# Where the weight splits of a fused attention and expert layer stand in their engines' queues

## The chip, the cores and the metric

The kernel runs on one core of a Trainium2 chip. The metric is the device time of one execution in microseconds (us). A core has five engines, each with a queue of its own: TensorE (PE) multiplies matrices, VectorE (DVE), ScalarE (ACT) and GpSimd (POOL) do elementwise work, SyncE (SP) issues the DMAs here.

## The reference

Two stages run one after the other. The first is attention with a decay per key, over 4 batches, 8 heads, 576 positions and a head size of 64. The second is a weighted sum of 4 dense experts over the 2304 rows of the attention's result, with 512 columns in and out and 1024 hidden columns.

```
scores = where(causal, -1e9, q @ k.T / sqrt(64) + cum[:, None] - cum[None, :])   # cum: running sum of log f
attn   = softmax(scores);  x = attn @ v                                          # then reshaped to (2304, 512)
h      = maximum(x @ w1[e], 0);  out += p[:, e] * (h @ w2[e])                    # e = 0..3, p normalized
```

All data are float32. The kernel keeps the precision by splitting an operand into a high part that TensorE can take and a low part (what is left), and by multiplying high by high, high by low and low by high.

## The kernel before

The result of the attention is cut into 9 chunks of 256 rows. The expert layer goes through chunks in small pieces that are called steps. A step is (s, g, c, ps): sweep s, group g of four weight units (two groups to an expert), chunk c, and ps, which of the two pairs of units of the group it uses. A unit is 128 hidden columns of one expert: 128x512 of w1 and 128x512 of w2, together 512 KB. Sweep 0 has the units 0 to 31 in a wide format, sweep 1 has the same weights again as units 32 to 63 in float16. `SWEEPS` says which chunks each sweep runs for each expert, and so how many chunks stand in a group: 1, 1, 2, 3 for the four experts of sweep 0, and 4, 4, 3, 2 for those of sweep 1. There are 28 steps in sweep 0 and 52 in sweep 1.

In the program's order, step n emits its first product (`l1`, 24 matmuls, line 1010), its gate (line 1023 on ACT takes the positive part as the high part, line 1024 on DVE makes the low part), and then the second product of step n-1 (`l2`, 12 matmuls, line 1043). Between these pieces `pace` emits slices of the attention for the chunks that come later: scores on PE (line 615), a running minimum on DVE (line 629), the exponential on ACT (line 644), normalized parts on ACT and DVE (lines 713 and 714), a transposing DMA, and the product with v (line 815). The preparation of a head is a copy of its q and k on ACT (line 562) and three instructions on POOL: line 563, line 571 (low part of k) and line 577 (low part of q), in `prep_lo`. Line 563 writes a buffer that the score matmuls of an earlier head read.

Each unit is loaded into one of three raw buffers (line 935, on SP's queue) and then split by `w_split`. For a unit of sweep 1 that is five instructions: line 977 on ACT and line 978 on DVE for the half of w1, line 969 on POOL, line 972 on ACT and line 973 on POOL for the half of w2. Splitting unit n also asks for the loads of units n+1 to n+3, and two steps later for the store of the split unit to DRAM (line 986), where the last stage of the kernel reads it again. For units of sweep 0 it is line 950 on ACT and line 954 on DVE or POOL.

The loop over steps asks for the split of two units when the last step that uses an older pair has been emitted: after the step in `ends[w0]`, units w0+6 and w0+7. The order in which instructions stand in each engine's queue is then set by a scheduler at build time: it simulates the engines with a cost model and takes, at each engine, what is ready first and was asked for first. So an instruction can come to stand in front of others that were asked for earlier. The engines run their queues in that order. `tc.issue_after(i)` tells the scheduler that what is emitted inside must stand behind instruction i in the queue of i's engine, if it is on that engine; it adds no instruction. Already used in the kernel before is this:

```python
def behind(f_):
    with tc.issue_after(prev.last.ins):
        f_()
```

After the steps, a last stage (`Big`, `Second`) computes the chunks 5 to 8 together, with weights that are read back from DRAM or summed anew on POOL (lines 1175, 1207, 1341). Its first two weight pairs are asked for early by `first_units`, after the steps of units 54 and 58; they use the raw buffers too.

Of the kernel before, what the change touches and what calls it, by code (L numbers as in the profile page):

```python
# [25 lines left out]
SWEEPS = (  # L26
    ((0,), (0,), (0, 1), (0, 1, 2)),
    ((1, 2, 3, 4), (1, 2, 3, 4), (2, 3, 4), (3, 4)),
)
# [7 lines left out]
LAST = (5, 6, 7, 8)  # L37
EARLY = (54, 58)
AHEAD = 4
W_SLOT = (4, 6)  # L40
NEAR = 2
JOBS = ((0, 0), (1, 0), (2, 0), (3, 0), (0, 1), (1, 1), (2, 1), (3, 1))
# [36 lines left out]
def fused(ctx: ExitStack, tc: tile.TileContext, qk, v, f, probs, w, out):  # L79
# [110 lines left out]
    def at_step(n, f):  # L190
        later.setdefault(n, []).append(f)
# [47 lines left out]
    def behind(f):  # L239
        if prev is None:  # L240
            f()
            return
        with tc.issue_after(prev.last.ins):
            f()
# [248 lines left out]
    class Job:  # L493
# [71 lines left out]
        def prep_lo(self, hh):  # L565
            if hh not in self.kl:
                self.rows(hh)
            wq, wk, ko, qo = self.wq, self.wk, self.ko, self.qo
            r, hi, kl = self.raw[hh], self.hi[hh], self.kl[hh]
            eng = nc.vector if self is jobs[0] else nc.gpsimd  # L570
            eng.tensor_tensor(  # L571
                out=kl[:64, :wk],
                in0=r[:64, ko : ko + wk],
                in1=hi[:64, ko : ko + wk].bitcast(F32),
                op=ALU.subtract,
            )
            eng.tensor_tensor(  # L577
                out=hi[64:128, qo : qo + wq],
                in0=r[64:128, qo : qo + wq],
                in1=hi[64:128, qo : qo + wq].bitcast(F32),  # L580
                op=ALU.subtract,
            )

        def prep(self, hh):
            self.prep_hi(hh)
            self.prep_lo(hh)
# [287 lines left out]
                )  # L874


    zs, pts = [], []
    jobs = []
    for b, half in JOBS:
        for pr in range(NPR):  # L880
# [51 lines left out]
    def w_load(n):  # L932
        if n < NS and n not in wraw:
            wraw[n] = wr_p.tile([128, 1024], F32, tag="wr", name=f"wr{n}")
            nc.sync.dma_start(out=wraw[n], in_=w[n % 32])
# [3 lines left out]
    def w_pair(name):  # L939
        t = w_p.tile([128, 2, 1024], F16, tag=("wh", "wl")[len(pairs) % 2], name=name)  # L940
        pairs.append(t)
        return t

    def w_split(n):
        w_load(n)
        r = wraw.pop(n)
        if n < 32:
            wh[n] = w_p.tile([128, 1024], F32R, tag="wh", name=f"wh{n}")
            wl[n] = w_p.tile([128, 1024], F32R, tag="wl", name=f"wl{n}")
            nc.scalar.activation(out=wh[n], in_=r, func=AF.Copy)  # L950
            eng = nc.vector if n in W_DVE else nc.gpsimd
            for a in (0, 512):
                z = a + 512
                eng.tensor_tensor(  # L954
                    out=wl[n][:, a:z],
                    in0=r[:, a:z],
                    in1=wh[n][:, a:z].bitcast(F32),
                    op=ALU.subtract,
                )
        else:  # L960
            e = n % 32 // 8
            assert ("w", e) in known
            t = w_pair(f"w{n}")
            wh[n], wl[n] = t[:, 0], t[:, 1]
            for k in range(2):
                c = slice(512 * k, 512 * k + 512)
                sc = wsc[:, e, k : k + 1]
                if k == 1:
                    nc.gpsimd.tensor_scalar(  # L969
                        out=r[:, c], in0=r[:, c], scalar1=sc, scalar2=None, op0=ALU.mult  # L970
                    )
                    nc.scalar.activation(out=wh[n][:, c], in_=r[:, c], func=AF.Copy)
                    nc.gpsimd.tensor_tensor(
                        out=wl[n][:, c], in0=r[:, c], in1=wh[n][:, c], op=ALU.subtract
                    )
                    continue
                nc.scalar.activation(out=wh[n][:, c], in_=r[:, c], func=AF.Copy, scale=sc)
                nc.vector.scalar_tensor_tensor(
                    out=wl[n][:, c],
                    in0=r[:, c],  # L980
                    scalar=sc,
                    in1=wh[n][:, c],
                    op0=ALU.mult,
                    op1=ALU.subtract,
                )
            at_step(step + 2, lambda: nc.sync.dma_start(out=wd[n - 32], in_=t))
        w_load(n + 1)
        w_load(n + 2)
        w_load(n + 3)
# [196 lines left out]
    def split_1(p):  # L1186
        if p >= 16:
            return ()
        r = raw_half(p, 0)
        t, u = (  # L1190
            w_p.tile([128, 2, 1024], F16, tag="wh", name=f"b{k}{p}") for k in ("w", "s")
        )
        one = t.rearrange("p n (s f) -> p n s f", s=2)
        for n in range(2):
            nc.sync.dma_start(out=one[:, n], in_=wd[2 * p + n][:, :, :512])
        bw[p] = one, u.rearrange("p s (k f) -> p s k f", k=4)
        f = sums(f"wt{p}", r, SUMS)
        hi, lo = u[:, 0], u[:, 1]

        def scale(a):  # L1200
            x = f[:, a : a + 512]
            nc.scalar.activation(out=x, in_=x, func=AF.Copy, scale=wsc[:, p // 4, 0:1])  # L1202

        def part(a):
            x, h = f[:, a : a + 512], hi[:, a : a + 512]
            nc.scalar.activation(out=h, in_=x, func=AF.Copy)  # L1206
            nc.gpsimd.tensor_tensor(out=lo[:, a : a + 512], in0=x, in1=h, op=ALU.subtract)  # L1207

        return (
            lambda: scale(0),  # L1210
            lambda: (part(0), scale(512)),
            lambda: part(512),
        )

    def first_units(w0):
        if w0 in EARLY:
            for f_ in split_1(EARLY.index(w0)):
                f_()
# [311 lines left out]
    def upto(n):  # L1530
        nonlocal at
        while at < n:
            asteps[at][1]()
            at += 1
# [6 lines left out]
    goals = sorted((max(n - LEAD, 1), cost[need[c]]) for c, n in first.items() if n > 0)  # L1541
    goals.append((len(steps) - AHEAD, cost[-1]))
    while goals:
# [17 lines left out]
    def startup():  # L1561
# [13 lines left out]
        for s in range(FIRST + 2):  # L1575
# [24 lines left out]
            if s >= 5 and s % 2 == 1:  # L1600
                heads[s - 4][0].fin()
            if s in W_SLOT:
                w_split(W_SLOT.index(s))

    prev, step = None, 0
# [8 lines left out]
    j.begin(0)  # L1614
    for n in range(len(W_SLOT), 6):
        w_split(n)

    used = set()
    for n in range(len(steps) + 1):
        step = n  # L1620
        cur = steps[n] if n < len(steps) else None
        for f_ in later.pop(n, ()):
            behind(f_)
        for e, first_ in enumerate(PEEK):
            if 0 <= n - first_ < 16:
                w_peek(e, n - first_)
            if n == first_ + 17:
                a_, b_ = w_scale(e)
                behind(a_)
                at_step(n + 3, b_)  # L1630
        if 0 <= n - V_PEEK < NV:
            v_peek(n - V_PEEK)
        if n == V_PEEK + NV + 1:
            a_, b_ = v_scale()
            behind(a_)
            at_step(n + 2, b_)
        if cur is not None:
            if cur.c not in used:
                used.add(cur.c)
                upto(need[cur.c])  # L1640
            for c, m in TURN:
                if n >= m and c not in yh and ("x", c) in known:
                    narrow(c)
            if cur.s == 1:
                assert cur.c in yh
                weigh(cur.g // 2, cur.c)
            for q in range(4):
                cur.l1(q)
                pace(n + q / 8)
            cur.gate()  # L1650
        else:
            upto(len(asteps))
            chunks.close()
            late.h = late.enter_context(tc.tile_pool(name="h", bufs=4, side="right"))
            for e in range(E):
                weigh(e, LAST[0])
            big = [Big(p) for p in range(16)]
            turns = in_turns(0)
            for _ in range(3):
                next(turns)()  # L1660
        if prev is not None:
            for q in range(4):
                prev.l2(q)
                pace(n + (q + 4) / 8)
                if cur is None:
                    for _ in range(2 if q == 3 else 1):
                        next(turns)()
            for w0, t in ends.items():
                if t is prev:
                    if w0 + 7 < NS:  # L1670
                        w_split(w0 + 6)
                        w_split(w0 + 7)
                    first_units(w0)
        prev = cur

    for p in range(2):
# [88 lines left out]
```

## Time and profile before

| what | value |
|---|---|
| time, median of 3 runs | 936.33 us (935.25 to 938.32) |
| profiled execution | 940.96 us, span 939.2 us |
| mean granted TensorE clock | 0.976 |
| busy in the span: PE, DVE, ACT, POOL | 884.8, 718.5, 567.5, 523.7 us (94, 77, 60, 56%) |
| sweep 0, sweep 1, last stage | to about 240 us, to about 625 us, to the end |

The table is from the page of one profiled execution. Busy is the time in which an engine executes; a wait for a semaphore is idle time of the engine. In the rows further down, what stands in square brackets behind an instruction is the time that its engine sat idle in front of it and the instruction that released it. A granted clock of 1.00 is 2.4 GHz, 0.50 is 1.2 GHz, and what is between is a mixture over the stretch.

### The profile page before, as it was taken

What the parts mean: (1) busy time and instruction counts of PE and PEld (TensorE: products, weight loads), DVE (VectorE), ACT (ScalarE), POOL (GpSimd) and SP (SyncE); (2) the same over time, 40 slices, a digit from 0 to 9 for tenths busy, and PEclk for the clock granted to TensorE, in tenths of its full rate; (3) what the DMA queues carried; (4) which work ended last, traced back from release to release, by engine and by line L of the source; (5) the groups of instructions that cost most, each with busy time, mean ns of one, the idle gap of its engine ahead of it and who ended that gap; (6) DMA issues with size and microseconds to landing.
All of it is one profiled execution on the core that took longest, in us unless ns stands there. A gap on an engine that the chain in (4) does not pass through costs nothing.

```text
span 939.2 us, 16651 instructions
## 1 busy us (share of the span) xinstructions
PE 884.8 (94%) x5783; PEld 618.9 (66%) x5783; DVE 718.5 (77%) x1458; ACT 567.5 (60%) x1137; POOL 523.7 (56%) x528
## 2 busy tenths in 40 slices
PE   4899999999988999899899999999998999999998
PEld 3699998998755656676566656654455664566547
DVE  5768777786899988789887777576768756786487
ACT  5869766465577667567766676355665345653350
POOL 4666866567533564227752674165778627785060
PEclk9689999999989999999999999999999999999999
DMA  7458855647889799977999698514322423232003
GB/s 263 147 166 308 273 139 172 199 134 235 258 245 184 161 298 217 251 160 160 327 289 183 138 304 219 141 58 146 131 91 79 149 68 120 83 106 75 23 1 91
DMA packets 147508, 159.45 MB, mean 170 GB/s; under 512 B 86148, under 2 KB 107328, under 8 KB 147424
## 3 DMA queue, kind: packets, MB, share of 16 engines
q1 hardware_dynamic: 147424, 158.39, 60.8%
q8 instruction: 45, 0.74, 0.3%
q14 instruction: 39, 0.32, 0.1%
HBM read 117.30 MB, written 21.65 MB: 148 GB/s over the span
## 4 chain that ended last, share of the span: by engine, by line
PE 23%; POOL 13%; DVE 6%; ACT 5%; issue 4%; DMA 2%; POOLq 0%; DVEq 0%; ACTq 0%
PE y L1281 6%; PE m L1281 5%; PE l L1043 5%; POOL s L1341 5%; PE l L1010 4%; POOL wt L1175 4%; POOL wu L1175 2%; DMA wr<-in_w 2%; POOL bs L1207 1%; PE s L615 1%; DVE acc L1070 1%; POOL wr L969 1%; PE o L815 1%; DVE rl L1162 1%; ACT wt L1202 1%
## 5 line engine op out<-in xcount | busy, mean ns | idle before, releaser
L1010 PE MATMUL l<-y,w 128*128 128x256 f16 x1248 | 154.7, 273 | 1.1 <-DVE gl L1024 1.1
L644 ACT ACTIVATE p<-p,nm 128x576 f32<-128x576 f32 (+3 forms) x160 | 95.6, 598 | 72.9 <-DVE nm L629 63.4
L1010 PEld LDWEIGHTS <-w 128*128 128x128 f16 x1248 | 117.7, 98 | 33.3 <-issue 8.9
L1043 PE MATMUL l<-w,gh 128*128 128x512 f16 x408 | 125.1, 390 | 6.9 <-DVE acc L1070 5.3
L714 DVE SCALAR_TENSOR_TENSOR z<-p,rs,z 128x384 f16<-128x384 f32 (+3 forms) x128 | 92.0, 743 | 9.3 <-ACT z L713 7.3
L615 PE MATMUL s<-hi 128*128 128x384 f32 (+1 forms) x192 | 75.5, 397 | 20.6 <-DVE hi L577 8.8
L563 POOL CAST q<-raw 64x320 fp32r<-64x320 f32 (+1 forms) x56 | 26.6, 476 | 120.0 <-PE s L615 79.5
L1070 DVE SCALAR_TENSOR_TENSOR acc<-y,scg,acc 128x256 f32<-128x256 f32 (+1 forms) x164 | 81.1, 515 | 14.9 <-PE y L1281 14.7
L571 POOL TENSOR_TENSOR kl<-raw,hi 64x576 fp32r<-64x576 f32 (+1 forms) x56 | 65.3, 1166 | 39.4 <-ACT hi L562 38.6
L1281 PE MATMUL m<-rh,bs 128*128 128x512 f16 x256 | 86.4, 379 | 0.0
L629 DVE CUSTOM_DVE_ANT_0 p<-s,mask 128x288 f32<-128x288 f32 (+2 forms) x160 | 74.7, 474 | 13.1 <-PE s L615 12.4
L1207 POOL TENSOR_TENSOR bs<-wt,bs 128x512 f16<-128x512 f32 x32 | 38.4, 1202 | 78.2 <-ACT bs L1206 78.0
L1043 PE MATMUL l<-w,gl 128*128 128x512 f16 x204 | 78.5, 390 | 2.0 <-DVE gl L1024 2.0
L969 POOL TENSOR_SCALAR wr<-wr,wsc 128x512 f32<-128x512 f32 x32 | 54.5, 1708 | 36.5 <-DMA wr<-in_w 36.0
L713 ACT ACTIVATE z<-p,rs 128x384 f16<-128x384 f32 (+3 forms) x128 | 69.5, 589 | 6.6 <-DVE rs L675 4.5
L954 POOL TENSOR_TENSOR wl<-wr,wh 128x512 fp32r<-128x512 f32 x48 | 63.1, 1339 | 12.5 <-ACT wh L950 6.9
L1010 PE MATMUL l<-xh,wh 128*128 128x256 f32 x224 | 66.5, 299 | 0.8 <-ACT xh L856 0.8
L1043 PEld LDWEIGHTS <-gh 128*128 128x128 f16 x408 | 37.2, 100 | 44.6 <-issue 14.2
L1024 DVE SCALAR_TENSOR_TENSOR gl<-l,gh 128x512 f16<-128x512 f32 (+1 forms) x80 | 54.7, 684 | 15.0 <-ACT gh L1023 14.4
L1010 PE MATMUL l<-xl,wh 128*128 128x256 f32 x224 | 66.2, 295 | 0.0
L1010 PE MATMUL l<-xh,wl 128*128 128x256 f32 x224 | 65.7, 293 | 0.1
L1281 PE MATMUL m<-rh,bw 128*128 128x512 f16 x191 | 64.4, 379 | 1.4 <-ACT r L1327 1.4
(385 smaller groups left out, 2349.0 us busy)
## 6 DMA issues: line engine op xcount, KB each, us to landing
wr<-in_w SPq DMA_DIRECT2D x90, 512.0 KB
pk<-in_w SPq DMA_DIRECT2D x64, 256.0 KB
wd<-w SPq DMA_DIRECT2D x32, 512.0 KB
raw<-in_qk SPq DMA_DIRECT2D x32, 448.0 KB
bw<-wd SPq DMA_DIRECT2D x32, 256.0 KB
bv<-wd SPq DMA_DIRECT2D x32, 256.0 KB
raw<-in_qk SPq DMA_DIRECT2D x24, 256.0 KB
vp<-in_v SPq DMA_DIRECT2D x10, 512.0 KB
```

The costliest lines, as they stand in the source:

```text
L571: eng.tensor_tensor(out=kl[:64, :wk], in0=r[:64, ko : ko + wk], in1=hi[:64, ko : ko + wk].bitcast(F32), op=ALU.subtract,)
L615: nc.tensor.matmul(out=ps[:, at : at + z - a], lhsT=lhsT, rhs=rhs, start=(m == 0), stop=(m == 1),)
L629: nc.vector.tensor_tensor_reduce(out=pt[:, a:z], in0=ps, in1=mask[:, m0 + a : m0 + z], scale=-0.125, scalar=BIG if n == 0 else nm[:, col : ...
L644: nc.scalar.activation(out=pt[:, :w_], in_=pt[:, :w_], func=AF.Exp, scale=-1.0, bias=self.nmax[hh][:, c : c + 1], accum_out=self.ssum[:, h ...
L713: nc.scalar.activation(out=o[:, 0], in_=x, func=AF.Copy, scale=sc)
L714: nc.vector.scalar_tensor_tensor(out=o[:, 1], in0=x, scalar=sc, in1=o[:, 0], op0=ALU.mult, op1=ALU.subtract)
L954: eng.tensor_tensor(out=wl[n][:, a:z], in0=r[:, a:z], in1=wh[n][:, a:z].bitcast(F32), op=ALU.subtract,)
L969: nc.gpsimd.tensor_scalar(out=r[:, c], in0=r[:, c], scalar1=sc, scalar2=None, op0=ALU.mult)
L1010: nc.tensor.matmul(out=self.l1p[:, fi, :], lhsT=lhsT, rhs=rhs[:, k, :], start=(k == 0 and m == 0), stop=(k == 3 and m == 2),)
L1043: matmul(out=l2[tt], lhsT=lhsT, rhs=rhs, start=(self.ps == 0 and fi == 0 and m == 0), stop=(self.ps == 1 and fi == 1 and m == 2),)
L1070: nc.vector.scalar_tensor_tensor(out=acc[c][:, tt, d0:d1], in0=ps, scalar=sc, in1=acc[c][:, tt, d0:d1], op0=ALU.mult, op1=ALU.add,)
L1281: line.append(nc.tensor.matmul(**args))
```

## The change

Three things are changed. First, everything that a call of `w_split` in the loop over steps emits is put behind three instructions, each on its own engine: on ACT behind the current step's gate (line 1023), on DVE behind the low part of the gate (line 1024), on POOL behind the low part of q of the head that was prepared last (line 577, which `prep_lo` now notes in `lows`). Second, the two units that are asked for at the end of a second pair (ps = 1) are asked for 0, 1, 2 or 3 steps later, where the group has 1, 2, 3 or 4 chunks. Third, the splits are now emitted after `first_units`, not ahead of it. The first six units, which are split ahead of the loop, stay as they were.

```diff
+REST = (0, 0, 1, 2, 3)
...
-            eng.tensor_tensor(
+            i = eng.tensor_tensor(
                 out=hi[64:128, qo : qo + wq],
                 in0=r[64:128, qo : qo + wq],
                 in1=hi[64:128, qo : qo + wq].bitcast(F32),
                 op=ALU.subtract,
             )
+            if self is not jobs[0]:
+                lows.append(i)
...
-    zs, pts = [], []
+    zs, pts, lows = [], [], []
...
-    used = set()
+    def paced(t, f):
+        with tc.issue_after(t.first.ins), tc.issue_after(t.last.ins), tc.issue_after(lows[-1].ins):
+            f()
+
+    used, splits = set(), {}
...
             for w0, t in ends.items():
                 if t is prev:
                     if w0 + 7 < NS:
-                        w_split(w0 + 6)
-                        w_split(w0 + 7)
+                        wait = REST[len(SWEEPS[t.s][t.g // 2])] if t.ps else 0
+                        splits.setdefault(n + wait, []).extend((w0 + 6, w0 + 7))
                     first_units(w0)
+            for m in splits.pop(n, ()):
+                paced(cur or prev, lambda: w_split(m))
         prev = cur
```

## Rows read from the trace of the kernel before

**Rows 1.** The page's first part, TensorE: busy us, share of the span, instructions.

```profile
PE 884.8 (94%) x5783; PEld 618.9 (66%) x5783; DVE 718.5 (77%) x1458; ACT 567.5 (60%) x1137; POOL 523.7 (56%) x528
```

**Rows 2.** Stretches of both sweeps: busy us by engine, granted clock, DMA share, GB/s.

```profile
60.00:240.00 180.00, 177.10 (x1199) 161.95 (x1197) 136.22 (x329) 120.64 (x267) 121.30 (x133) 0.99 0.67 210
240.00:300.00 60.00, 54.16 (x356) 36.94 (x354) 55.25 (x122) 41.22 (x86) 27.57 (x26) 0.94 0.93 228
300.00:500.00 200.00, 186.94 (x1362) 127.19 (x1360) 171.28 (x374) 136.95 (x276) 98.71 (x91) 0.98 0.94 233
500.00:580.00 80.00, 76.92 (x568) 52.17 (x568) 63.24 (x143) 56.46 (x114) 44.14 (x40) 0.98 0.85 210
580.00:625.00 45.00, 44.47 (x320) 29.16 (x317) 33.21 (x53) 19.23 (x36) 16.40 (x15) 1.00 0.46 113
```

**Rows 3.** The timeline of TensorE: matmuls with idle time in front of them.

```profile
264.92 0.61 PE L615 MATMUL s<-hi 128*128 128x288 f32 x1 [4.54 <-DVE nm L629]
...
325.62 0.49 PE L1010 MATMUL l<-y,w 128*128 128x256 f16 x3 [1.08 <-DVE gl L1024]
...
334.55 0.50 PE L615 MATMUL s<-hi 128*128 128x512 f32 x1 [1.62 <-DVE ux L203]
...
459.01 1.01 PE L1043 MATMUL l<-w,gh 128*128 128x512 f16 x2 [2.68 <-DVE acc L1070]
...
549.97 0.39 PE L1043 MATMUL l<-w,gl 128*128 128x512 f16 x1 [1.98 <-DVE gl L1024]
```

**Rows 4.** Waits of ACT, DVE, POOL, 240 to 600 us: total, times, longest.

```profile
ACT w L977 <- DMA wr<-in_w: 24.6, 8, 6.6
...
ACT w L972 <- POOL wr L969: 1.5, 3, 1.0
...
DVE w L978 <- ACT w L977: 13.5, 11, 2.6
...
POOL q L563 <- PE s L615: 44.8, 8, 13.4
```

**Rows 5.** Stretches around three of the waits, columns as in rows 2.

```profile
260.00:280.00 20.00, 15.46 (x92) 9.16 (x90) 18.53 (x40) 14.41 (x31) 6.09 (x6) 0.83 0.86 238
440.00:480.00 40.00, 37.11 (x267) 25.20 (x262) 35.52 (x72) 30.82 (x63) 30.60 (x25) 0.96 0.99 272
540.00:560.00 20.00, 18.02 (x125) 11.43 (x124) 16.30 (x32) 14.35 (x29) 16.05 (x12) 0.91 1.14 321
```

**Rows 6.** The timeline of ACT: two splits that wait for their load.

```profile
256.24 0.72 ACT L977 ACTIVATE w<-wr,wsc 128x512 f16<-128x512 f32 x1 [4.89 <-DMA wr<-in_w]
...
332.61 0.72 ACT L977 ACTIVATE w<-wr,wsc 128x512 f16<-128x512 f32 x1 [6.59 <-DMA wr<-in_w]
```

**Rows 7.** Instructions of a split by line, 240 to 600 us: busy, mean ns.

```profile
L978 DVE SCALAR_TENSOR_TENSOR w<-wr,wsc,w 128x512 f16<-128x512 f32 x28 | 26.8, 973 | 13.5 <-ACT w L977 13.5
...
L969 POOL TENSOR_SCALAR wr<-wr,wsc 128x512 f32<-128x512 f32 x26 | 45.2, 1740 | 27.9 <-DMA wr<-in_w 27.6
...
L973 POOL TENSOR_TENSOR w<-wr,w 128x512 f16<-128x512 f32 x28 | 35.5, 1282 | 9.7 <-ACT w L972 8.7 <-POOL hi L577 0.4 <-DMA pk<-in_w 0.2
...
L977 ACT ACTIVATE w<-wr,wsc 128x512 f16<-128x512 f32 x28 | 19.4, 714 | 25.3 <-DMA wr<-in_w 24.6 <-PE l L1043 0.5 <-DVE wsc L293 0.2
...
L972 ACT ACTIVATE w<-wr 128x512 f16<-128x512 f32 x28 | 17.1, 620 | 1.6 <-POOL wr L969 1.5
```

**Rows 8.** The timeline of ACT: the gates of steps 33, 43 and 46.

```profile
296.01 0.57 ACT L1023 ACTIVATE gh<-l 128x512 f16<-128x512 f32 x1
...
375.18 0.59 ACT L1023 ACTIVATE gh<-l 128x512 f16<-128x512 f32 x1
...
392.78 0.58 ACT L1023 ACTIVATE gh<-l 128x512 f16<-128x512 f32 x1
```

**Rows 9.** The timelines of POOL and DVE: the splits of units 40 to 42.

```profile
318.35 4.94 POOL L969 TENSOR_SCALAR wr<-wr,wsc 128x512 f32<-128x512 f32 x3
...
318.65 2.68 DVE L978 SCALAR_TENSOR_TENSOR w<-wr,wsc,w 128x512 f16<-128x512 f32 x3 [0.94 <-ACT w L977]
```

## The prediction, before the changed kernel was run

> **What bounds the kernel now.** I read the page first: TensorE is busy for 884.8 of 939.2 us [rows 1], so its idle time is 54 us in all. Cutting the span into stretches shows where such waits lie. Sweep 0 has few, 2.9 us in the 180 before 240 us, but sweep 1 between 240 and 580 us has them: PE is busy 54.16 + 186.94 + 76.92 = 318.0 of 340 us, so 22.0 us are idle; from 580 to 625 us only 0.5 us is [rows 2]. The view of what ended PE's idle time names DVE almost everywhere, and DVE is itself busy for 92% of 240 to 300 and about 85% of the next 280 us [rows 2]. That could be read as "DVE is the bound". The waits of the other engines say more. From 240 to 600 us ACT stands for 24.6 us, in 8 places, at line 977, the first instruction of a split, until that unit's load lands; DVE stands 13.5 us behind it at line 978 [rows 4]. Both run their queues in order, so gates, exponentials and minima behind the split stand too.
>
> The timeline shows how this reaches PE. At 251.35 ACT comes to the split of unit 39 (the eighth instruction of line 977, counted from unit 32) and stands 4.89 us until 256.24 [rows 6]. All that is queued on ACT comes late, then DVE with its minima, and at 264.92 PE stands 4.54 us for a minimum on DVE [rows 3]. Unit 43 does the same: ACT stands 6.59 us until 332.61 [rows 6], and PE 1.62 us at 334.55 [rows 3]. The splits of 40 to 42 had come in one block at 318.35 [rows 9], and PE stands 1.08 us at 325.62. With the blocks of units 48 to 53 and 56 to 62 go the waits of 2.68 us at 459.01 and 1.98 us at 549.97 [rows 3]. It is nearly always the fourth unit of a block that waits: three raw buffers hold three loaded units, and the fourth load starts when the first of them has been split.
>
> None of this hurry is needed. Unit 39 is asked for behind step 33, whose gate runs at 296.01, unit 43 behind step 43, gate at 375.18 [rows 8]; they ran about 40 us ahead of these places [rows 6]. The scheduler pulls a split forward as soon as its simulated load is there, and on the chip the load is later.
>
> **The price of these waits.** The five rows add to 4.54 + 1.08 + 1.62 + 2.68 + 1.98 = 11.9 us [rows 3]. After the larger ones TensorE's granted clock falls for a while to the lower of its two levels: the mean is 0.83 over 20 us, 0.96 over 40 and 0.91 over 20 [rows 5], which costs 0.17 x 20 + 0.04 x 40 + 0.09 x 20 = 6.8 us of work. Together 18.7 us hang on blocks of splits; the other 22.0 - 11.9 = 10.1 us of idle time come without one.
>
> **The change part by part.** (1) The order edges add and remove no instruction. A unit of sweep 1 costs 0.714 + 0.620 us on ACT, 0.973 on DVE and 1.740 + 1.282 on POOL [rows 7], before and after. What moves is their place: behind the gate of the step that asks for them. For the splits that ran there already (most of sweep 0, where a slot of the split unit comes free only then) nothing changes, and I cost that at nothing; PE is full there.
>
> (2) Nine pairs go one to three steps later still: units 24, 28 by one, 32, 36, 56, 60 by two, 44, 48, 52 by three, each with its neighbour. Two pairs then come no longer in successive steps, so the fourth load has two steps or more to land: three steps take 392.78 - 375.18 = 17.6 us [rows 8], two about 11.7, against a longest wait of 6.6 [rows 4]. I expect ACT's 24.6 us at line 977 to fall below 8.
>
> (3) Is a split late for its use? Units 42 and 43, now behind gate 43, are first used in step 45. Their half of w1 is needed by its first product, a step and a half or 8.8 us later; it takes two instructions on ACT and two on DVE, 3.4 us. Their half of w2 is needed after 17.6 us [rows 8]; POOL takes 2 x (1.740 + 1.282) = 6.0 us [rows 7] and the preparation of a head ahead of it. So the margin covers it. If POOL's preparation is itself held, as it is at line 563 for up to 13.4 us [rows 4], that cover is gone: the second rival.
>
> (4) The loads, and the stores two steps after a split, move along on SP's queue past transposes and loads of q, k and v. They were released by the same splits before, and three buffers are loaded well ahead, so I take nothing; at the other end one landing in the open, bounded by 6.6 us [rows 4]. There is one such place: units 60 and 61 now come behind step 74 and 62, 63 behind step 75, and the first weight pair of the last stage now takes a raw buffer ahead of unit 63. ACT is busy for only 19.2 of 45 us there and POOL 16.4 [rows 2]; four units add 4 x 3.02 = 12.1 us to POOL, which fits. I take 1.5 us of loss between 0 and 6.6.
>
> (5) DVE decides how much of the 18.7 us comes back. Between 240 and 300 us the share is 4.54 + 3.4 = 7.9 us, but DVE has only 60 - 55.25 = 4.75 us free [rows 2], and units 34 and 35, which ran before 240, move in with 2 x 0.973 = 1.9. So 2.8 us at most; I take it. Of the other 10.8 us I take two thirds, 7.2: DVE has 28.7 + 16.8 = 45.5 us free in those 280 us [rows 2], but its own backlog stands in these chains as well. The ends are 0 and 10.8.
>
> **A rule that would speak against it.** Behind the gate, line 978 always meets POOL's line 969. While three instructions of line 969 ran without a break, three of line 978 took 2.68 us, 0.89 each [rows 9], against a mean of 0.973 [rows 7]: no loss. The Trainium skill (SBUF — State Buffer, section Who interferes with whom) says that a VectorE instruction with two SBUF inputs contends with a GpSimd instruction that reads SBUF, and that the loser is blocked for the other's whole duration. By that rule each of these would stand up to 1.74 us; by the row the sum gains nothing from it and loses nothing.
>
> **The sum.** 2.8 + 7.2 - 1.5 = 8.5 us off the profiled 940.96 gives 932.5. The runs before have a median of 936.33, 4.6 us under the profiled one, so I predict 927.8.
>
> **Rivals.** *DVE takes the place of ACT.* With ACT free, DVE at 85 to 92% is the next to be late, or the changed order makes new waits like the 10.1 us that have no split behind them; the gain stays under 2.8 us: about 935. For it: every wait in rows 3 names DVE as the last releaser. Against it: DVE itself stands 13.5 us for the splits [rows 4].
>
> *Slower: ACT stands at line 972 in place of line 977.* Line 972 needs line 969 on POOL, and that now stands behind line 577, whose head must first pass line 563; there POOL stands 44.8 us in 8 places, at most 13.4 [rows 4]. So ACT would be held by POOL in the middle of a split, with the next gate behind it. 24.6 us of standing cost 18.7, or 0.76 us each. With 14 pairs in 240 to 600 us, 24.6 / 14 = 1.8 us a pair gives back all, and over 2.0 it is slower. At 2.3 us a pair: 32.2 x 0.76 - 18.7 = 5.8 us, 942. Against it: ACT stood only 1.5 us at line 972, in 3 places [rows 4]. The skill's page TensorE: Matmul & The Clock Gate, section Architectural detail, calls ACT and DVE strict FIFO, as rows 6 bear out; this rival lives on it.
>
> *DVE held by POOL*, the rule above as a mechanism: were each of the 28 instructions of line 978 held half of line 969, 0.87 us, it would be 24 us of DVE, priced as ACT's 0.76: 927.8 + 18.5 = 946. Rows 9 speak against it.
>
> *More than forecast:* over 2.8 + 10.8 = 13.6 us back, up to all 18.7, so 922 or less.
>
> **Chances and range.** Forecast 0.56, DVE in place of ACT (or edges that change nothing) 0.18, ACT at line 972 0.17, line 978 held 0.03, more than forecast 0.06. So faster by over 0.3% (2.8 us, about what a measurement of this kernel can tell) 0.56 + 0.06 = 0.62, within 0.3% 0.18, slower 0.17 + 0.03 = 0.20. The range 916 to 943 takes in the full 18.7 us below and the milder half of the slower rival above; the forecast's own range is 922 (13.6 us back, nothing lost) to 933 (2.8 us back).
>
> **What would show it.** Right: ACT's wait at line 977 for loads under 8 us, splits in pairs and each behind its gate (unit 43 behind step 43), the wait of 4.54 us gone, and a granted clock near 1.00 from 260 to 280 us. Wrong: ACT standing at line 972, PE standing in front of line 1010 or 1043 for lines 973 or 978, PE's idle time in sweep 1 still near 22 us with DVE over 90% busy, or a gap between 590 and 635 us behind the late splits.

## The result and the profile after

The changed kernel takes 926.14 us (median of 4 runs, 923.96 to 930.58) beside 936.83 us for the kernel before; the ratio is 0.9895, 95% interval 0.9855 to 0.9935. The prediction was 927.8 us, so sign and size came out. The terms of its sum did not, as the stretches show. Every line number from line 40 on is 1 to 3 higher now: of the split, line 977 is 980, 978 is 981, 969 is 972, 972 is 975 and 973 is 976; 1010 is 1013 and 1043 is 1046.

The page's engines, and then the stretches with the columns of [rows 2]:

```profile
PE 882.4 (95%) x5783; PEld 620.7 (67%) x5783; DVE 710.0 (76%) x1458; ACT 569.3 (61%) x1137; POOL 528.0 (57%) x528
```

```profile
60.00:240.00 180.00, 172.16 (x1142) 155.96 (x1142) 132.54 (x332) 118.83 (x263) 113.82 (x130) 0.97 0.62 195
240.00:300.00 60.00, 57.25 (x419) 43.68 (x418) 52.98 (x120) 45.27 (x93) 30.49 (x26) 1.00 0.90 221
300.00:500.00 200.00, 195.09 (x1418) 132.97 (x1415) 173.46 (x388) 137.84 (x279) 97.60 (x90) 0.99 0.96 232
500.00:580.00 80.00, 80.00 (x604) 55.13 (x604) 66.78 (x143) 56.98 (x115) 44.59 (x37) 1.00 0.91 218
580.00:625.00 45.00, 41.79 (x265) 24.99 (x264) 30.12 (x43) 23.20 (x40) 35.33 (x33) 0.96 0.58 206
```

I call idle time of PE plus (1 - granted clock) x length the lost time of a stretch; the clock has two digits, so it is good to about 1 us in 200. Before [rows 2] and after it is:

| stretch | before | after | forecast of the difference | measured |
|---|---|---|---|---|
| 60 to 240 | 2.90 + 1.8 = 4.7 | 7.84 + 5.4 = 13.2 | 0 | 8.5 lost |
| 240 to 300 | 5.84 + 3.6 = 9.4 | 2.75 + 0 = 2.8 | 2.8 won | 6.7 won |
| 300 to 580 | 16.14 + 5.6 = 21.7 | 4.91 + 2.0 = 6.9 | 7.2 won | 14.8 won |
| 580 to 625 | 0.53 + 0 = 0.5 | 3.21 + 1.8 = 5.0 | 1.5 lost | 4.5 lost |

Together 8.5 us, the sum of the forecast, by terms of which none is right; the span fell by 10.4 us. Sweep 1 won more than twice what I took, and sweep 0 and the tail lost much of it again.

Each stretch is of one execution, and that of the changed kernel (930.58 us) is the slowest of its four. How far one execution can be off shows in two kernels of the experiments, the first one of "The tail" and "Four units behind one gate": up to 300 us their queues hold the same instructions in the same order as those of the changed kernel, on every engine. From 60 to 240 us they read, in this order:

```profile
60.00:240.00 180.00, 173.87 (x1165) 157.25 (x1163) 134.68 (x345) 122.06 (x271) 117.31 (x131) 0.99 0.63 203
60.00:240.00 180.00, 173.06 (x1173) 157.16 (x1171) 135.27 (x345) 122.98 (x273) 117.67 (x132) 1.00 0.64 203
```

They lost 7.9 and 6.9 us there, in place of 13.2. The queues of the kernel before ran a second time too, up to 445 us ("the delays without the edges"), and lost 2.2 us in place of 4.7. So a term of the table is good to a few us: sweep 0 lost between 2 and 11 us by the change, and that the four terms add to just the forecast's sum is chance.

The waits answer to [rows 4] and [rows 7]: the groups of a split by line, 240 to 600 us. The last part of a row is the idle time in front of these instructions.

```profile
L972 POOL TENSOR_SCALAR wr<-wr,wsc 128x512 f32<-128x512 f32 x30 | 50.6, 1692 | 7.7 <-DMA wr<-in_w 5.8 <-DVE ux L204 0.6
L976 POOL TENSOR_TENSOR w<-wr,w 128x512 f16<-128x512 f32 x32 | 40.7, 1280 | 31.8 <-ACT w L975 31.6
L981 DVE SCALAR_TENSOR_TENSOR w<-wr,wsc,w 128x512 f16<-128x512 f32 x30 | 34.0, 1155 | 1.5 <-ACT w L980 1.4
L980 ACT ACTIVATE w<-wr,wsc 128x512 f16<-128x512 f32 x30 | 20.2, 712 | 0.1
L975 ACT ACTIVATE w<-wr 128x512 f16<-128x512 f32 x31 | 18.8, 617 | 0.1
```

ACT's 24.6 us in front of the first half of w1 are 0.1 us, DVE's 13.5 us behind it 1.4. The five waits of [rows 3] are gone, and the clock of [rows 5] with them:

```profile
260.00:280.00 20.00, 20.00 (x164) 14.62 (x162) 18.49 (x37) 16.43 (x33) 10.39 (x10) 1.00 0.78 208
440.00:480.00 40.00, 40.00 (x301) 27.82 (x300) 34.69 (x77) 27.84 (x57) 18.95 (x17) 1.00 1.06 277
540.00:560.00 20.00, 20.00 (x153) 13.86 (x152) 17.19 (x37) 13.69 (x30) 13.04 (x9) 1.00 0.96 219
```

What stands there now is in the timeline: the two large waits of TensorE that are new in sweep 0, what led to the first of them on POOL, ACT and DVE, and the largest waits of sweep 1 and of the tail.

```profile
112.06 0.39 POOL L564 CAST q<-raw 64x256 fp32r<-64x256 f32 x1 [3.70 <-PE s L618]
...
115.34 5.02 POOL L957 TENSOR_TENSOR wl<-wr,wh 128x512 fp32r<-128x512 f32 x4
...
117.89 0.33 SPq L938 DMA_DIRECT2D wr<-in_w  x1
...
123.14 1.06 ACT L953 ACTIVATE wh<-wr 128x1024 fp32r<-128x1024 f32 x1 [4.62 <-DMA wr<-in_w]
...
124.48 0.47 ACT L754 ACTIVATE pt<-t 128x384 fp32r<-128x384 f32 x1
...
124.98 0.56 DVE L761 TENSOR_TENSOR pt<-t,pt 128x384 fp32r<-128x384 f32 x1 [4.73 <-ACT pt L754]
...
125.60 0.48 PE L744 MATMUL t<-ident,p 128*128 128x128 f32 x1 [3.20 <-DVE pt L761]
...
230.66 0.27 PE L200 MATMUL topx<-ident,xmax 128*1 128x128 f32 x1 [2.73 <-DVE xmax L261]
...
296.75 1.69 PE L818 MATMUL o<-pt,v 128*64 128x320 f16 x27 [2.75 <-DMA pt<-z]
...
322.14 2.17 PE L818 MATMUL o<-pt,v 128*64 128x320 f16 x27 [2.23 <-DMA pt<-z]
...
412.24 0.59 PE L1046 MATMUL l<-w,gh 128*128 128x512 f16 x2 [1.65 <-DVE acc L1073]
...
591.84 0.39 PE L1013 MATMUL l<-y,w 128*128 128x256 f16 x2 [1.90 <-ACT w L980]
```

Read from the top, this is the hazard of [rows 6] once more, in sweep 0: POOL waits 3.70 us to prepare a head, so the low halves of the split units (line 957) stand behind it until 115.34, their raw buffers come free late, the next load is issued at 117.89, and ACT stands 4.62 us at a split (line 953) with a copy for DVE behind it, and TensorE 3.20 us behind that. In the kernel before, POOL made the low halves of the same two units (18 and 19) about 11 us earlier:

```profile
104.51 5.06 POOL L954 TENSOR_TENSOR wl<-wr,wh 128x512 fp32r<-128x512 f32 x4
```

The edge on POOL put line 957 behind the head. How much hangs on this chain differs from one execution to the next: in the two kernels with the same queues TensorE's wait there is 1.08 and 0.98 us (at 123.10 and 123.47 us), while the wait of 2.73 us at line 200 comes in both, with 2.72. Whether the edge is the cause was left to a run.

### The profile page after: what moved, and what is told of

It is laid out like the page before. It is cut to its first block, busy times and chain, and to the rows that moved or that the text cites. A ratio compares the mean times of both kernels' runs of the same rounds, so it can differ in the third digit from the quotient of the medians.

```text
span 928.8 us, 16629 instructions
## 1 busy us (share of the span) xinstructions
PE 882.4 (95%) x5783; PEld 620.7 (67%) x5783; DVE 710.0 (76%) x1458; ACT 569.3 (61%) x1137; POOL 528.0 (57%) x528
## 4 chain that ended last, share of the span: by engine, by line
PE 55%; POOL 12%; DVE 10%; ACT 7%; DMA 7%; issue 4%; SPq 0%; ACTq 0%; POOLq 0%; DVEq 0%
PE l L1046 16%; PE l L1013 15%; PE y L1284 8%; PE m L1284 7%; PE s L618 4%; POOL s L1344 4%; POOL wt L1178 3%; PE o L818 2%; POOL wu L1178 1%; DMA wr<-in_w 1%; DMA pk<-in_w 1%; DVE acc L1073 1%; DVE z L717 1%; DMA vr<-in_v 1%; ACT wt L1205 1%
## 5 line engine op out<-in xcount | busy, mean ns | idle before, releaser
L1046 PE MATMUL l<-w,gh 128*128 128x512 f16 x408 | 122.2, 382 | 2.7 <-DVE acc L1073 2.0
L717 DVE SCALAR_TENSOR_TENSOR z<-p,rs,z 128x384 f16<-128x384 f32 (+3 forms) x128 | 82.4, 665 | 12.7 <-ACT z L716 11.3
L618 PE MATMUL s<-kl,q 66*128 66x384 f32 (+1 forms) x192 | 63.2, 334 | 2.2 <-DMA kl<-nc 2.2
L1284 PEld LDWEIGHTS <-bs 128*128 128x128 f16 x384 | 37.6, 98 | 38.4
```

Of the source, the lines that this page charges most:

```text
L618: nc.tensor.matmul(out=ps[:, at : at + z - a], lhsT=lhsT, rhs=rhs, start=(m == 0), stop=(m == 1),)
L717: nc.vector.scalar_tensor_tensor(out=o[:, 1], in0=x, scalar=sc, in1=o[:, 0], op0=ALU.mult, op1=ALU.subtract)
L1046: matmul(out=l2[tt], lhsT=lhsT, rhs=rhs, start=(self.ps == 0 and fi == 0 and m == 0), stop=(self.ps == 1 and fi == 1 and m == 2),)
L1284: line.append(nc.tensor.matmul(**args))
```

## The experiments

Each is told by its difference from the changed kernel, unless it says otherwise. The kernel before, timed beside them in three sets, took 936.95, 937.36 and 938.65 us; ratios are to the set's own.

**The edges without the delays.**

```diff
-REST = (0, 0, 1, 2, 3)
+REST = (0, 0, 0, 0, 0)
```

> The order edges are kept, every delay is 0. Theory (the gain of sweep 1 comes from the edges and the delays together: edges keep a split from running ahead, delays leave the fourth load time to land): four units are asked for in two successive steps about 6 us apart, so the fourth still meets its load at the head of ACT's queue; ACT waits 8 to 15 us in all for loads at the first half of w1 between 240 and 600 us (0 in the changed kernel, 24.6 before), about half of the 21 us of sweep 1 is lost again, and the time is about 930 to 934 us. Rival 1 (the edges alone do it): no load waits, 926 us. Rival 2 (the tail's loss comes from the delay of units 60 to 63): the wait of TensorE near 592 us goes, 3 us back, about 923 us.

Measured: 939.29 us, ratio to before 1.0031 (1.0012 to 1.005). **The delays without the edges**, `f()` in place of the three nested edges in `paced`:

> The delays are kept, the order edges are taken out, so the scheduler may again put a split in front of what was asked for earlier. Theory: the simulated engines are free and the simulated load is there, so splits run ahead in blocks as before; ACT waits 15 to 25 us for loads, TensorE idles about 20 us in 240 to 580 us, and sweep 0 is as it was before the change (under 5 us lost); the time is 931 to 939 us. Rival (the delay alone leaves the loads time): ACT waits under 8 us for loads, and with sweep 0 as before the change the time is 915 to 920 us.

Measured: 943.30 us, 1.0059 (1.0036 to 1.0081). Either half alone is slower than the kernel before. ACT's waits between 240 and 600 us are about what the theories said (8 to 15 and 15 to 25 us); first the edges alone, then the delays alone:

```profile
ACT w L980 <- DMA wr<-in_w: 15.5, 5, 4.7
```

```profile
ACT w L980 <- DMA wr<-in_w: 21.7, 8, 6.4
```

With edges alone ACT meets late loads again, and with delays alone it stands nearly as in the kernel before (24.6 us). The times are worse than I expected of both. The stretches of the edges alone say why:

```profile
60.00:240.00 180.00, 167.51 (x1110) 150.76 (x1109) 128.24 (x321) 119.14 (x262) 115.63 (x129) 0.98 0.59 189
240.00:300.00 60.00, 58.08 (x405) 44.73 (x404) 54.13 (x123) 42.17 (x86) 30.88 (x27) 1.00 0.89 233
300.00:500.00 200.00, 190.22 (x1392) 129.35 (x1391) 167.92 (x376) 133.87 (x272) 89.72 (x85) 0.98 0.93 222
```

In sweep 1 they lose 1.9 us from 240 to 300 and 13.8 us from 300 to 500 (after: 2.8 and 6.9), about a third of the way back to the 26.5 us of the kernel before, where half was expected; but sweep 0 loses 16.1 us, more than any execution with the changed kernel's queues (6.9 to 13.2). So the edges cost sweep 0, and the delays, whose part in sweep 0 I had not looked at, take some of that away. The delays alone change no engine's order in the first 445 us: sweep 0 with its 177.82 of 180 us is the kernel before once more, and so are the blocks of splits up to there. What is worse than before lies mostly in the tail:

```profile
580.00:625.00 45.00, 41.72 (x289) 27.91 (x288) 28.78 (x48) 17.31 (x34) 13.00 (x12) 0.96 0.50 146
```

There 3.28 + 1.8 = 5.1 us are lost, before 0.5.

**Edges and delays in sweep 1 alone.**

```diff
-                        wait = REST[len(SWEEPS[t.s][t.g // 2])] if t.ps else 0
+                        wait = REST[len(SWEEPS[t.s][t.g // 2])] if t.ps and w0 + 6 >= 32 else 0
...
-                paced(cur or prev, lambda: w_split(m))
+                paced(cur or prev, lambda: w_split(m)) if m >= 32 else w_split(m)
```

> Edges and delays for the units of sweep 1 alone (32 to 63); the units of sweep 0 are split as in the kernel before. Theory (the edges cost sweep 0 about 8.5 us, since raw buffers come free later behind POOL's preparation and ACT then stands for a load): sweep 0 loses under 5 us between 60 and 240 us, sweep 1 keeps what it won, and the time is 916 to 919 us. Rival (what sweep 0 lost is a new arrangement of TensorE's waits that has no link to its splits, or is given back in sweep 1): 925 to 927 us.

Measured: 926.17 us, 0.9895 (0.9867 to 0.9922), as the rival had it. Sweep 0 did come back (179.21 of 180 us busy at a clock of 1.00), but sweep 1 lost about as much: 21.0 us from 240 to 580 us, where the changed kernel lost 9.7. ACT stood 6.1 us for loads at line 980 from 240 to 600 us, in 3 places, and DVE 8.1 us at line 285, in 2. One place of it, in the stretches and the timeline:

```profile
300.00:500.00 200.00, 190.94 (x1390) 130.34 (x1390) 167.78 (x382) 137.35 (x279) 92.32 (x87) 0.97 0.92 228
```

```profile
317.13 0.55 SPq L282 DMA_DIRECT2D pk<-in_w  x1
...
322.70 0.69 DVE L285 TENSOR_REDUCE wmax<-pk 128x1 f32<-128x512 f32 x1 [5.01 <-DMA pk<-in_w]
...
323.31 1.21 DVE L261 TENSOR_REDUCE xmax<-xf 128x1 f32<-128x1024 f32 x1
...
324.57 0.37 PE L200 MATMUL topx<-ident,xmax 128*1 128x128 f32 x1 [4.32 <-DVE xmax L261]
```

The same hazard on a third instruction: DVE stands 5.01 us at a maximum over raw weights (line 285) for a load issued at 317.13, and TensorE 4.32 us behind it. The wait of 2.73 us at 230.66 in the changed kernel ends on the same two lines of DVE.

**Only POOL's edge out of sweep 0.** Edges on ACT and DVE and all delays stay.

```diff
-        with tc.issue_after(t.first.ins), tc.issue_after(t.last.ins), tc.issue_after(lows[-1].ins):
-            f()
+        with tc.issue_after(t.first.ins), tc.issue_after(t.last.ins):
+            with tc.issue_after(lows[-1].ins) if m >= 32 else nullcontext():
+                f()
```

> As the changed kernel, but the units of sweep 0 are not held behind POOL's preparation of a head; their edges on ACT and DVE and the delays stay. Theory (POOL's edge frees the raw buffers late, so ACT stands for loads in sweep 0): ACT's waits for loads at the split of sweep 0 fall from 7.9 us to about 4 us, TensorE's idle time from 60 to 240 us from 7.8 to under 4 us; the total is 922 to 926 us, as sweep 1 may take it back. Rival (the edges on ACT and DVE cost it): idle time in sweep 0 stays at 6 to 9 us.

Measured: 920.34 us (918.17 to 921.69), 0.9817 (0.9794 to 0.9839), the fastest of all and better than the theory's range. Its stretches:

```profile
60.00:240.00 180.00, 180.00 (x1227) 165.26 (x1226) 144.44 (x357) 124.66 (x275) 115.10 (x131) 1.00 0.65 201
240.00:300.00 60.00, 55.15 (x399) 38.14 (x398) 54.73 (x110) 46.01 (x95) 34.80 (x28) 0.97 1.03 245
300.00:500.00 200.00, 194.89 (x1447) 133.17 (x1445) 174.24 (x392) 139.38 (x283) 97.39 (x90) 1.00 0.93 232
500.00:580.00 80.00, 78.36 (x585) 52.85 (x582) 62.22 (x131) 51.43 (x104) 45.05 (x40) 1.00 0.80 204
580.00:625.00 45.00, 42.99 (x237) 23.78 (x238) 29.30 (x43) 25.45 (x44) 32.71 (x30) 0.96 0.69 241
```

Sweep 0 has no idle time at all; the lost time is 0, 6.7, 5.1 + 1.6 and 3.8 us. Three further kernels below leave this edge out of sweep 0, and in each TensorE is busy for 180.00 of 180 us; in the five with it, it is 167.51 to 173.87. So it is POOL's edge, not those on ACT and DVE, that cost sweep 0; and of what sweep 0 won 5.8 us show in the time, unlike with edges and delays in sweep 1 alone. The path is less sure than the cause. ACT's longest wait for a load in sweep 0 is 2.0 us in place of 4.6, but the sum of these waits from 60 to 240 us fell only from 7.9 to 6.3 us, where about 4 was expected, and in the kernel before ACT's waits for loads there add to 8.5 us (4.1 at line 950 and 4.4 at line 977), with little idle time of TensorE.

**No edge on POOL anywhere.** The `lows` edge is left out of `paced`.

> As the changed kernel, but no unit is held behind POOL's preparation of a head; the edges on ACT and DVE and the delays stay for all units. With POOL's edge taken away for sweep 0 alone TensorE was full in sweep 0 and the time 920.3 us. Theory (in sweep 1 POOL's edge is neutral, since POOL's part of a split has a margin there): sweep 0 stays full (under 2 us idle of 180) and the time is 918 to 923 us. Rival (in sweep 1 POOL's edge is worth something, since without it the scaling for the second half of a unit runs ahead and stands on POOL for a load, with a preparation behind it): POOL's waits for loads at that line rise from 5.8 to over 10 us, 924 to 930 us.

Measured: 923.28 us, 0.9852 (0.9826 to 0.9877). The runs (922.71 to 925.79) lie above all of those with POOL's edge in sweep 1 alone, but they are of another set and the two intervals overlap. POOL's wait for loads at line 972, 240 to 600 us, and one place:

```profile
POOL wr L972 <- DMA wr<-in_w: 28.2, 11, 6.3
```

```profile
275.21 1.56 POOL L972 TENSOR_SCALAR wr<-wr,wsc 128x512 f32<-128x512 f32 x1 [6.92 <-DVE v L551]
...
278.22 1.06 POOL L578 TENSOR_TENSOR hi<-raw,hi 64x320 fp32r<-64x320 f32 x1
...
279.33 0.69 PE L618 MATMUL s<-hi 128*128 128x384 f32 x1 [3.16 <-POOL hi L578]
```

The rival is right on the wait: without the edge line 972 runs ahead and stands on POOL (28.2 us for loads, 5.8 in the changed kernel), with the preparation of a head behind it. In the place shown TensorE waits 3.16 us for the preparation; the profile puts POOL's 6.92 us there down to an instruction of DVE, not to a load. The time lies between the two ranges: in sweep 1 the edge is worth about 3 us, at the edge of what these runs can tell, and in sweep 0 it cost more. The run also answers a rival that was not named: POOL stands for loads as long as in the kernel before (27.6 us at line 969 [rows 7]), ACT not at all at line 980, and the time is 15 us under the kernel before. So POOL's standing had cost at most a small part of this.

**The maxima behind their gate**, once in the changed kernel and once with edges and delays in sweep 1 alone: the reduction of line 285 wrapped in `behind`.

> As the changed kernel, and the maxima over the raw weights that DVE takes ahead of sweep 1 (64 of them, each behind a load of 256 KB) now stand behind the gate of the step before. Theory (such a maximum is the same hazard as a split: it stands at the head of DVE's queue for a load that is late): DVE's wait for that load of 2.9 us goes, and with it TensorE's wait of 2.7 us near 230 us and some clock; 921 to 924 us. Rival (another link of the chain takes the place): 925 to 928 us.

> Edges and delays for the units of sweep 1 alone, and the maxima over the raw weights behind the gate of the step before. With the first alone sweep 0 was full (0.8 us idle of 180), but in sweep 1 DVE stood 8.1 us for the loads of these maxima, and TensorE 4.3 us behind it near 325 us. Theory (what sweep 0 wins is lost to this one hazard): both waits go, 4.3 us of idle time and 3 to 5 us of clock come back, 917 to 921 us. Rival (sweep 1 is bound by the sum of DVE's work and of the transposes on SP's queue, so any wait that is taken away comes up elsewhere): 924 to 928 us.

Measured: 925.84 us (0.9855 to 0.9899 of before) and 927.78 us (0.9884 to 0.9924): no gain, both theories fell. DVE still stood 2.8 and 9.4 us for these loads from 60 to 640 us, and TensorE's waits for the maximum were 2.72 and 3.31 us. The edge did not take away the wait for the load. That these waits are what sweep 1 lost is so only argued.

**The tail.** Units 60 and 61 undelayed (`if t.ps and w0 < 54`), and the loop with `paced` ahead of the one with `first_units`; first in the changed kernel, then in the fastest one, then also with loads of half the size as below.

> As the changed kernel, but units 60 and 61 are not delayed and the splits are again emitted ahead of the first weight pairs of the last stage. Theory (the waits near 592 us come from units 60 to 63 being split two steps late, behind a weight pair that takes a raw buffer): TensorE no longer waits for the first half of w1 there, the 3 to 4 us of the tail come back, 922 to 924 us. Rival (the tail's waits are the head of the last stage and come wherever the splits stand): 926 us.

> Without POOL's edge for the units of sweep 0, and with units 60 and 61 not delayed and the splits emitted ahead of the first weight pairs of the last stage. Theory (the two losses are independent): the wait of 2.2 us for the first half of w1 in the tail goes, and what hangs on it, 917 to 920 us. Rival (the tail's order only moves its wait to the last stage): 920 to 922 us.

> The second kernel of this list, with each load of a unit cut into two of 256 KB, the half of w1 first. Theory (a load wait at the head of ACT's queue is no longer on the path, so a load that lands earlier gives nothing, where it gave 4.5 us in the kernel before): within 2 us of the second kernel. Rival (the waits that are left in sweep 0 and sweep 1 still hang on loads): 3 us or more under it.

Measured: 925.59, 923.20 and 923.54 us. TensorE's wait at line 1013 near 590 us (580 in the fastest) went in all three, and no time with it: the first is where its rival had it, the second 2.9 us above the fastest kernel and above both ranges. In the second one stands instead, with a transfer and the last stage's first operands late:

```profile
577.59 2.66 PE L818 MATMUL o<-pt,v 128*64 128x320 f16 x23 [3.26 <-DMA pt<-z]
...
607.88 0.38 PE L1284 MATMUL m<-rh,bs 128*128 128x512 f16 x1 [0.76 <-ACT rh L1164]
609.62 0.38 PE L1284 MATMUL m<-rl,bs 128*128 128x512 f16 x1 [1.37 <-DVE rl L1165]
```

Smaller loads gave nothing on top of the second, as expected.

**The kernel before with each load in two halves,** so that no split is moved by hand and only the wait gets shorter:

```diff
-            nc.sync.dma_start(out=wraw[n], in_=w[n % 32])
+            for a in (0, 512):
+                nc.sync.dma_start(out=wraw[n][:, a : a + 512], in_=w[n % 32, :, a : a + 512])
```

> The kernel before, with each load of a unit cut into two of 256 KB, the half of w1 first; splits stand where the scheduler puts them, without edges or delays. Theory (it is the load at the head of ACT's queue that costs, not the place of the split as such): the half that ACT needs first lands earlier, ACT's waits for loads fall from 24.6 us to 10 to 18 us, and the time falls by a third of the 18.7 us that hang on them, to 929 to 934 us. Rival (waits are due to when the load is released, and the doubled number of transfers on SP's queue costs as much): 935 to 942 us.

Measured: 932.84 us, 0.9954 (0.9926 to 0.9982), against 937.36. Line 978 of this kernel is line 977 of the kernel before. ACT's waits fell less than expected, the longest from 6.6 to 4.9 us:

```profile
ACT w L978 <- DMA wr<-in_w: 20.2, 8, 4.9
```

4.4 us less of standing and 4.5 us less time, 1.7 to 6.9 by the interval; by the prediction's price of 0.76 us for each it would be 3.3. Nine of its ten runs lie between 928.08 and 939.44 us (the tenth took 944.82), those of the kernel before between 935.02 and 941.77, so the size is less sure than the sign.

**Four units behind one gate.** `wait = 1 - t.ps` in sweep 1.

> As the changed kernel with all its edges, but in sweep 1 the four units that two successive steps ask for are split behind one gate, that of the second of these steps, with no further delay; sweep 0 is as in the changed kernel. Theory (the cost lies in the fourth unit meeting its load at the head of ACT's queue, since only three raw buffers hold loaded units): ACT waits 15 to 30 us for loads at the first half of w1 (15.5 with edges and no delays, 0 in the changed kernel), and the time is 932 to 938 us. Rival (it is enough that a split stands behind its gate): under 5 us of waits, 925 to 928 us.

Measured: 956.54 us, 1.0207 (1.0179 to 1.0236), slower than either expected, and not for the theory's reason: ACT waited 1.1 us for loads. The units did not stand at a load, and ACT did not take four in a row: unit 45 came at 380.01 us, 9 us behind unit 44 at 370.95. The last ones were split later: the first half of w1 of unit 63 came at 624.12 us on ACT (593.87 in the changed kernel):

```profile
577.50 2.74 PE L1013 MATMUL l<-y,w 128*128 128x256 f16 x12 [5.77 <-ACT w L980]
...
624.88 8.06 PE L1013 MATMUL l<-y,w 128*128 128x256 f16 x48 [7.28 <-ACT w L980]
```

So this run prices a split that is late for its use, 5.77 and 7.28 us and a clock of 0.80 from 580 to 625 us, and says nothing of the load.

## Why the prediction came out, point by point

- **What costs, and the mechanism** were right for sweep 1. ACT's 24.6 us and TensorE's five waits went together, a run that only shortened the wait (halved loads) won time without moving a split by hand, and a run in which POOL stood for the loads of splits in sweep 1 and ACT did not was 15 us under the kernel before. Neither half of the change did it alone: the delays changed nothing in the first 445 us and left 21.7 us of standing, and the edges left 15.5 us, lost about half as much in sweep 1 (240 to 580 us) as the kernel before, and paid for it in sweep 0. Edges without delays and without POOL's edge in sweep 0 were not tried, so what the delays are worth there is open.
- **Part (1), "For the splits that ran there already (most of sweep 0, where a slot of the split unit comes free only then) nothing changes, and I cost that at nothing", failed.** Sweep 0 lost 8.5 us by the profiled executions, 2 to 11 by all with these queues. On POOL the splits had not run there already: units 18 and 19 stood ahead of the next preparation. I named the edge on POOL and what stands ahead of it, but looked only at the margin of sweep 1, where a group has up to four chunks. Sweep 0 splits two units a step while a group has one chunk, and there POOL's half decides when a raw buffer comes free (unit 18 was done at 117.86 us, the next load issued at 117.89). The run without this edge in sweep 0 has a full TensorE there and is 5.8 us faster.
- **Part (3), POOL's margin in sweep 1, held.** ACT stood 0.1 us in all at line 975 (972 before) between 240 and 600 us, so the slower rival was not there; POOL itself stood 31.6 us in front of line 976, but no wait of TensorE from 240 to 580 us ends on POOL.
- **Part (5), 2.8 and 7.2 us, was mis-sized.** 240 to 300 us won 6.7, but that stretch is not the same work: the last gate of sweep 0 came at 239.59 us before and at 254.60 after. In the run with a full sweep 0 it won 9.4 - 6.7 = 2.7, close to the 2.8 of the cap by DVE's free time; from one execution that can be chance. From 300 to 580 us two thirds of 10.8 was too careful: 14.8 us were won, and 15.0 in that run, more than hung on splits by my count. So some of the waits that I had set aside, because no split stood behind them, or of the clock that I had not counted, seem to have gone as well; which of them is not shown.
- **Part (4), the tail, 1.5 us of 0 to 6.6, was mis-sized:** 4.5 us lost. The place was right (unit 61's half of w1, 1.90 us at 591.84), but undoing it moved the wait to the transposes and the last stage, so it is not 4.5 us that a better order would give back.
- **The rival with DVE in ACT's place** did not come for the total. In parts it did: from 240 to 580 us TensorE's waits that are left end on DVE or on a transposing transfer, and with edges and delays in sweep 1 alone TensorE's largest wait (4.32 us) came behind one of DVE at line 285; that this took back what sweep 0 had won is argued. Why the run without POOL's edge in sweep 0 kept it, where that one did not, stays open; the traces show that ACT stood 0.4 us for loads at line 980 here and 6.1 us there, and DVE 3.6 and 8.1 us at line 285.
- **The rule on DVE and POOL** I set aside with the wrong neighbour in view; see the last section. Its price as I worked it out (24 us of DVE) did not come either.

## What to carry to other kernels

An instruction that waits for a load stands at the head of an engine that runs its queue in order, so it is worth placing by the load's time on the chip, not by its readiness in a plan: here it took both, a place behind the urgent work and enough distance for the load. Check such an edge on every engine and in every phase by itself; here one edge of three cost about 6 us in one phase and was worth perhaps 3 in another. And read the stretches after a success too: here a right total was made of four wrong terms, by luck, and the one that I had put at nothing held the next 6 us. Where two kernels share their queues up to some point, compare them up to there: it shows how much one execution differs from the next.

## What the hardware did that was not expected

DVE's part of a split (line 981) became longer, 1155 ns on average after 973 [rows 7], 0.18 us for each of 30. The timeline shows beside what:

```profile
508.35 3.32 POOL L972 TENSOR_SCALAR wr<-wr,wsc 128x512 f32<-128x512 f32 x2
508.55 1.69 DVE L981 SCALAR_TENSOR_TENSOR w<-wr,wsc,w 128x512 f16<-128x512 f32 x2
...
564.58 2.72 POOL L976 TENSOR_TENSOR w<-wr,w 128x512 f16<-128x512 f32 x2 [7.79 <-ACT w L975]
564.65 3.20 DVE L981 SCALAR_TENSOR_TENSOR w<-wr,wsc,w 128x512 f16<-128x512 f32 x2
```

Beside line 972 on POOL, which reads one tensor, one takes 0.85 us; beside line 976, which reads two, 1.60 us, nearly twice as long. [rows 9] showed only the first case, so the prediction's "no loss" was drawn from the harmless neighbour. In the whole trace those that ran mainly beside line 972 took 0.74 to 1.03 us. Of the 12 mainly beside line 976 seven took 1.63 to 1.65 us, one 2.92, and four, of which 0.24 to 0.66 us ran beside it, 0.74 to 0.75. Beside lines 572 and 578, which prepare a head and read two tensors as well, some took 1.2 to 1.5 us. Line 976 itself took 1.40 us on average where it met line 981, and 1.19 where it did not.

The Trainium skill (SBUF — State Buffer, section Who interferes with whom) states the rule that the prediction set aside. This trace agrees with it for a POOL instruction with two SBUF inputs, by about 0.9 us (the one that ran beside nothing on POOL took 0.74) and not for the whole of the other's duration (1.28 us on average), and hardly for one with a single input. In this kernel DVE's longer part comes to about 5 us (30 x 0.18) from 240 to 600 us, and no wait of TensorE was traced to it.
